# Order of the first transfers and number of filler matmuls at the head of an FFT-convolution kernel

## The chip, the cores and the metric

The kernel runs on one core of a Trainium2 chip. The metric is device time in microseconds; lower is better. The time before is the median of three runs, 264.54 us (264.13 to 264.58).

## What is computed

A circular two-dimensional convolution of one 224 x 224 image with 96 channels in and 96 out, and a 7 x 7 filter. The reference does it by Fourier transforms:

```python
H = W = 224; C = 96; K = 7
wp = jnp.pad(w, ((0, H - K), (0, W - K), (0, 0), (0, 0)))
Xf = rfft2(x, axes=(1, 2))
Wf = rfft2(wp, axes=(0, 1))
Yf = jnp.einsum('bhwi,hwio->bhwo', Xf, Wf)
y = irfft2(Yf, s=(H, W), axes=(1, 2)).astype(bfloat16)
```

## The kernel before

The kernel does not follow the reference's transform over the whole image. Rows are cut into eight blocks of 28, each with a halo of 6 rows, and a short transform (17 slots of frequencies, `NS`) runs along the rows as a matmul with a table `Fm`. Along the columns the filter's taps are applied as shifted matmuls, with combinations of taps and planes that save multiplications. The image is walked in seven tiles of 32 columns (`t` = 0 to 6).

For one tile, stage A transforms pixels (`xn` and, for the first tile, a part of `WF` that is not yet needed) to `xf`; VectorE (DVE) makes sums and differences of planes of `xf`, called `J`, in `jit`; stage B (`b_round`, 17 rounds a tile) multiplies `xf` and `J` with the transformed filter `WF` and sums into `yf`; `yf` goes through DRAM (`scr`) and comes back as `tt`, on which stage C (`c_jobs`) transforms back with a table `Gm` and stores. PSUM is one pool of eight banks, and each matmul group takes the next bank (`bank()`). Which of VectorE and ScalarE (ACT) evacuates a bank is fixed when the program is built, by a running sum of costs (`evac`).

The wrapper `_Ordered` makes each engine, and the one DMA queue that SyncE (SP) issues, execute in the order in which the program is written. So the head is an order written by hand. These are its steps:

- L178 to L192, the transfers. `xh_bufs` are the 6 halo columns left of the first tile, for each of the two halves of the image's rows (`jg` 0 and 1). `load_x(0, 0)` loads the first tile's pixels of the first half, `load_x(0, 1)` (L197) those of the second. `load_rows` issues two transfers each, 112 rows and 6. The weights go to `wq`: two transfers for the last filter tap's row, three for a third of the columns of the other 48 rows. Then four transfers copy them within the chip, from even to odd partitions of `wq`, shifted by half the output channels; each copy waits for the weight transfer whose bytes it reads.
- L199 to L208, `warm(n)`: n matmuls of a zero tile `wu`, 512 columns wide, into a bank that nobody reads. They are the fillers; `warm(8)` and `warm(9)` stand ahead of everything on TensorE.
- L231 to L347: GpSimd (POOL), VectorE and ScalarE compute the tables `Fm` and `Em` (the filter's transform, columns behind the weights in `wq`), and POOL alone goes on to the table `Gm` (`build_g`), in small operations on tiles called `ct`. Its last two steps, a sine on ACT and a product on POOL, are in `fin` (L342), which L776 calls as `g_fin()`.
- L758 to L769, TensorE's head: 12 matmuls for the halo columns of both halves (`a_bank`), 96 for the first half of the first tile (`fj[p][0]`, jobs for three groups of frequencies), then the fillers of L766, then `prep_jobs(0)`, 48 matmuls of `wq` that give the first two slots of `WF`.
- L770 to L776: the second half's first group of jobs (`fj[0][1]`, 32 matmuls), the loads of the second tile's pixels, the first planes `J` (`jit(0, 0)`), and `g_fin()`.
- From L816 on, the rounds. The first round of stage B writes `tt__557` (a PSUM copy on ACT, L567), the second `tt__676` (ACT, L604) and `u` (DVE, L607). Between the rounds' matmuls run the other `prep_jobs` and the remaining jobs of the first tile.

Of the kernel before, what the change touches and what calls it, by code (L numbers as in the profile page):

```python
# [21 lines left out]
PAD = KT - 1  # L22
# [33 lines left out]
def kernel(  # L56
# [7 lines left out]
    _, H, W, C = x.shape  # L64
# [40 lines left out]
    def bank():  # L105
        return pools["psb"].tile([128, 512], F32, name="pb")
# [5 lines left out]
    def apart(key, zone, r):  # L112
        for z, q in parts.setdefault(key, []):
            if z != zone and q.engine != r.ins.engine:
                tc.declare_no_dep(r.ins, q, reason="disjoint parts of one tile")
        parts[key].append((zone, r.ins))
        return r

    def evac(out_ap, in_ap, n):
        if tail[0]:  # L120
            return tail_evac(out_ap, in_ap, n)
        cv, ca = 180 + 1.0 * n, 160 + 0.85 * n
        if load["v"] + cv <= load["a"] + ca:
            load["v"] += cv
            return VE.tensor_copy(out=out_ap, in_=in_ap)
        load["a"] += ca
        return SE.copy(out=out_ap, in_=in_ap)
# [5 lines left out]
    def dma(out_ap, in_ap):  # L133
        return DE.dma_start(out=out_ap, in_=in_ap)
# [26 lines left out]
    xh_bufs = [late[:, 2 * (XW + 32) + i * XHW:2 * (XW + 32) + (i + 1) * XHW] for i in range(2)]  # L161
    assert 2 * (XW + 32 + XHW) <= 8 * NTAP * C and NSLOT - 8 > slot(PGRP[-1][0], 0)

    def load_rows(xb, jg, w0, npx):
        h0 = jg * HB - PAD
        n = npx * C

        def ld(p0, p1, hh):
            return dma(xb[p0:p1, 0:n], x[0, hh:hh + (p1 - p0), w0:w0 + npx, :].rearrange("h w c -> h (w c)"))
        return ld(PAD, R, h0 + PAD), ld(0, PAD, h0 % H)  # L170

    def xbuf(t, jg):
        return (xn_bufs if t else x0_bufs)[jg]

    def load_x(t, jg):
        return load_rows(xbuf(t, jg), jg, t * 2 * TW, 2 * TW)

    wsrc = w.rearrange("kh kw i o -> (kh kw) (i o)")  # L178
    for jg in range(2):
        load_rows(xh_bufs[jg], jg, W - PAD, PAD)  # L180
    load_x(0, 0)
    cuts = tuple((c * WC // 3, (c + 1) * WC // 3) for c in range(3))
    lr = PW - 1
    wp = WC // 16
# [1 line left out]
                bass.AP(wsrc.tensor, wsrc.offset + lr * WC + h * wp, [[WC, 1], [2 * wp, 8], [1, wp]])) for h in range(2)]  # L186
    for c0, c1 in cuts:
        wdma.append(dma(wqx[0:2 * lr:2, c0:c1], wsrc[0:lr, c0:c1]))
    wdma.append(dma(wqx[2 * lr + 1:PW2, 0:WC - C2].rearrange("p (a b) -> p a b", a=16),
                    wqx[2 * lr:2 * lr + 1, C2:WC].rearrange("p (a b) -> p a b", a=16)))  # L190
    for c0, c1 in cuts:
# [11 lines left out]
    def warm(n):  # L203
        pwu = bank()
        for _ in range(n):
            TE.matmul(pwu[:].rearrange("p (a b) -> p a b", a=4), lhsT=wu[:, 0:128], rhs=wur, start=True, stop=True)
# [215 lines left out]
    def a_bank(t, xf, xb, px, n, jg, pos):  # L422
        def single(ph):
            def f():
                pa = bank()
                a_mm(pa, xb, px + ph, n)
                a_put(t, xf, pa, ph, n, jg, pos)
            return f

        def pair():  # L430
            pa = psum_tile()
            for ph in range(2):
                a_mm(pa[:, ph], xb, px + ph, n)
            a_put(t, xf, pa, slice(0, 2), n, jg, pos)
        return [pair] if t > 2 and NP2 else [single(0), single(1)]
# [18 lines left out]
    def f_jobs(t, part):  # L454
        s0, s1 = SH2[part], SH2[part + 1]
        n = 2 * (s1 - s0) * JG
        nr = -(-TW * n // 512)
        e = [-(-TW * i // nr) for i in range(nr + 1)]
        fv = Fm[:, :, s0:s1].rearrange("p r s j -> p r (s j)")

        def mk_(jg, a, b, ph):
            def f():
                pa = bank()
                for k in range(b - a):
                    i = 2 * (a + k) + ph
                    TE.matmul(pa[:, k * n:(k + 1) * n], lhsT=xbuf(t, jg)[:, i * C:i * C + 128], rhs=fv, start=True, stop=True)
                xo = xf_tiles[t][0:C, ph, :, s0:s1, HALO + a:HALO + b, jg * JG:(jg + 1) * JG]
                pi = pa[0:C, 0:(b - a) * n].rearrange("c (w r s j) -> c r s w j", r=2, s=s1 - s0, w=b - a)
                return apart(("A", t), (a, jg, ph, part), evac(xo, pi, (b - a) * n))
            return f  # L470
        return [[mk_(jg, a, b, ph) for a, b in zip(e[:-1], e[1:]) for ph in range(2)] for jg in range(2)]
# [287 lines left out]
    for jg in range(2):  # L759
        for f in a_bank(0, xf0, xh_bufs[jg], 0, 3, jg, 0):  # L760
            f()
    fj = [f_jobs(0, p) for p in range(3)]
    for p in range(3):
        for f in fj[p][0]:
            f()
    for n in (9, 9, 6):  # L766
        warm(n)
    for f in prep_jobs(0):
        f()  # L769
# [202 lines left out]
```

## Time and profile before

| | us |
|---|---|
| median of three runs | 264.54 |
| the profiled execution | 264.27 |
| its span | 262.6 |
| TensorE busy in the span | 253.1 |
| DVE / ACT / POOL busy | 214.2 / 198.4 / 105.4 |
| TensorE busy in the first 20 us | 18.94 |
| granted TensorE clock, mean over the span | 0.995 |

All profile lines of this document have the operation's source line as L88, the line of the wrapper, so operations are told apart by the tiles that they write and read. In a timeline the columns are the start in us from the span's start, the time in us, the engine, the line, the operation, out<-in by the program's names, the shapes, and the number of instructions; in brackets the engine's idle time before it and what ended it. TensorE appears as PE (matmul) and PEld (weight load), SP's queue as SPq. The chain of waits gives start, time and engine of the work that ended last, followed back from the end.

TensorE's own timeline of the head:

```profile
1.06 6.81 PE L88 MATMUL pb<-wu 128*128 128x512 bf16 x17 [1.06 <-DVE ct L88]
7.71 3.41 PE L88 MATMUL pb<-Fm,WF 118*128 118x136 bf16 x108
10.96 5.34 PE L88 MATMUL pb<-wu 128*128 128x512 bf16 x24
16.14 3.16 PE L88 MATMUL pb<-wq 98*128 98x128 bf16 x48
19.14 1.10 PE L88 MATMUL pb<-Fm,WF 118*128 118x64 bf16 x32
20.69 0.51 PE L88 MATMUL pb<-WF,xf 96*128 96x96 bf16 x8 [0.46 <-ACT xf L88]
```

The ends of matmuls are modelled, so one row can end after the next begins. Up to 20.69 no row but the first has idle time before it.

### The profile page before, as it was taken

To read this page: it belongs to the slowest core of one execution; us is meant where nothing else is said; L and a number is where in the kernel's file an instruction comes from. 1 tells how busy PE (TensorE), PEld (TensorE's weight loads), DVE (VectorE), ACT (ScalarE), POOL (GpSimd) and SP (SyncE) were. 2 spreads that over 40 slices of the span, in tenths; PEclk is the share of its full clock that TensorE was granted. 3 is DMA by queue.
4 is the path that set the end of the run, shared out by engine and by line. 5 is a ranking of instruction groups with operands and counts; after the bars stand their busy time and mean duration, and the time that the engine had idled before them with its cause. 6 is when DMAs were issued, how large, how long until landed. Compare 5 with 4: busy or idle time off the path is not lost.

```text
span 262.6 us, 12208 instructions
## 1 busy us (share of the span) xinstructions
PE 253.1 (96%) x5160; PEld 234.6 (89%) x5160; DVE 214.2 (82%) x456; ACT 198.4 (76%) x500; POOL 105.4 (40%) x170
## 2 busy tenths in 40 slices
PE   8999998999999999999999999999999999999982
PEld 2779898999999999998999998999999999999961
DVE  5648899897979969977888788777977889889982
ACT  5549997659785666998988869989798886666662
POOL 7783032336355452234123322443133221556621
PEclk9999999999999999999999999999999999999997
DMA  6847110541111399888978559598958854586135
GB/s 163 237 140 194 35 49 2 167 149 47 50 47 47 117 245 192 246 234 210 279 241 218 166 137 316 166 259 188 325 201 206 216 161 149 146 141 187 55 112 177
DMA packets 41416, 43.44 MB, mean 165 GB/s; under 512 B 30836, under 2 KB 33104, under 8 KB 41362
## 3 DMA queue, kind: packets, MB, share of 16 engines
q1 hardware_dynamic: 41044, 41.98, 57.9%
q8 instruction: 40, 0.66, 1.1%
q0 software_dynamic: 192, 0.52, 0.7%
q10 hardware_dynamic: 126, 0.17, 0.2%
q14 instruction: 14, 0.11, 0.1%
HBM read 22.09 MB, written 19.66 MB: 159 GB/s over the span
## 4 chain that ended last, share of the span: by engine, by line
PE 85%; DVE 4%; ACT 4%; issue 3%; POOL 1%; DVEq 0%; ACTq 0%
PE pb L88 85%; ACT WF L88 2%; DVE WF L88 1%; ACT xf L88 1%; DVE xf L88 1%; POOL yf L88 1%; DVE J L88 1%; DVE u L88 1%; DVE v L88 0%; DVE yf L88 0%; ACT tt L88 0%; ACT tt__676 L88 0%; ACT tt__2951 L88 0%; ACT tt__557 L88 0%; DVE wu L88 0%
## 5 line engine op out<-in xcount | busy, mean ns | idle before, releaser
L88 PE MATMUL pb<-WF,J 96*128 96x96 bf16 x2782 | 160.4, 206 | 0.4 <-DVE WF L88 0.3
L88 PEld LDWEIGHTS <-J 96*128 96x128 bf16 x2782 | 136.1, 98 | 8.6 <-DVE u L88 1.5
L88 POOL TENSOR_TENSOR yf<-v,u 128x384 bf16<-128x384 f32 x70 | 69.0, 1000 | 129.8 <-issue 69.3
L88 ACT CAST xf<-pb 96x408 bf16<-96x408 f32 (+3 forms) x143 | 67.2, 489 | 9.1 <-PE pb L88 7.4
L88 PE MATMUL pb<-WF,xf 96*128 96x96 bf16 x991 | 61.7, 206 | 1.1 <-ACT xf L88 0.5
L88 DVE TENSOR_TENSOR J<-xf 96x1824 bf16<-96x1824 bf16 (+1 forms) x82 | 56.8, 732 | 0.1
L88 PEld LDWEIGHTS <-xf 96*128 96x128 bf16 x991 | 49.0, 98 | 2.0 <-issue 1.0
L88 PE MATMUL pb<-Fm,xn 118*128 118x136 bf16 (+3 forms) x640 | 45.5, 199 | 0.9 <-DVE u L88 0.8
L88 ACT CAST WF<-pb 96x480 bf16<-96x480 f32 (+1 forms) x59 | 29.0, 573 | 5.1 <-PE pb L88 5.0
L88 PE MATMUL pb<-tt,Gm 102*84 102x384 bf16 (+1 forms) x132 | 32.1, 326 | 0.0
L88 PEld LDWEIGHTS <-xn 118*128 118x128 bf16 x640 | 30.4, 97 | 1.2 <-issue 1.1
L88 ACT CAST yo<-pb 84x384 bf16<-84x384 f32 (+1 forms) x66 | 28.2, 485 | 2.9 <-PE pb L88 2.9
L88 ACT CAST J<-pb 84x384 bf16<-84x384 f32 (+1 forms) x65 | 28.0, 485 | 2.8 <-PE pb L88 2.5
L88 DVE TENSOR_TENSOR J<-J 96x912 bf16<-96x912 bf16 (+2 forms) x41 | 22.5, 548 | 0.0
L88 PE MATMUL pb<-wq 98*128 98x120 bf16 (+1 forms) x288 | 21.3, 226 | 0.0
L88 PEld LDWEIGHTS <-wq 98*128 98x128 bf16 x288 | 19.5, 148 | 0.2
L88 POOL TENSOR_TENSOR xn<-v,u 128x384 bf16<-128x384 f32 x12 | 10.9, 923 | 9.3 <-DVE J L88 6.3
L88 PE MATMUL pb<-wu 128*128 128x512 bf16 x43 | 12.7, 462 | 1.1 <-DVE ct L88 1.1
L88 DVE TENSOR_TENSOR yf<-v,u 128x384 bf16<-128x384 f32 x20 | 11.4, 568 | 0.7
L88 PEld LDWEIGHTS <-Gm 102*84 102x84 bf16 (+1 forms) x132 | 11.1, 117 | 0.8
L88 PEld LDWEIGHTS <-wu 128*128 128x128 bf16 x43 | 4.8, 115 | 7.7 <-issue 3.9
L88 DVE CAST WF<-pb 96x480 bf16<-96x480 f32 (+1 forms) x13 | 7.5, 611 | 4.8 <-PE pb L88 4.7
(404 smaller groups left out, 260.0 us busy)
## 6 DMA issues: line engine op xcount, KB each, us to landing
scr<-yf SPq DMA_DIRECT2D x30, 288.0 KB
xn<-in_x_dram SPq DMA_DIRECT2D x12, 672.0 KB
tt<-scr SPq DMA_DIRECT2D x24, 336.0 KB
out_dram<-yo SPq DMA_DIRECT2D x12, 252.0 KB
out_dram<-J SPq DMA_DIRECT2D x12, 252.0 KB
tt<-scr SPq DMA_DIRECT2D x6, 288.0 KB
WF<-in_x_dram SPq DMA_DIRECT2D x2, 672.0 KB
scr<-yf SPq DMA_DIRECT2D x6, 192.0 KB
```

Of the source, the lines that this page charges most:

```text
L88: r = fn(*a, **k)
```

## The change

The five weight transfers are issued first. Behind them come the halo columns and the first half of the first tile's pixels, then the four on-chip copies, then, unchanged, the second half. In TensorE's order, four fillers are put between the halo columns' matmuls and the first half's, and three stand ahead of `prep_jobs(0)` where there were 24. Nothing that the kernel computes changes.

```diff
     wsrc = w.rearrange("kh kw i o -> (kh kw) (i o)")
-    for jg in range(2):
-        load_rows(xh_bufs[jg], jg, W - PAD, PAD)
-    load_x(0, 0)
     cuts = tuple((c * WC // 3, (c + 1) * WC // 3) for c in range(3))
...
     for c0, c1 in cuts:
         wdma.append(dma(wqx[0:2 * lr:2, c0:c1], wsrc[0:lr, c0:c1]))
+    for jg in range(2):
+        load_rows(xh_bufs[jg], jg, W - PAD, PAD)
+    load_x(0, 0)
     wdma.append(dma(wqx[2 * lr + 1:PW2, 0:WC - C2].rearrange("p (a b) -> p a b", a=16),
...
     for jg in range(2):
         for f in a_bank(0, xf0, xh_bufs[jg], 0, 3, jg, 0):
             f()
+    warm(4)
     fj = [f_jobs(0, p) for p in range(3)]
     for p in range(3):
         for f in fj[p][0]:
             f()
-    for n in (9, 9, 6):
+    for n in (3,):
         warm(n)
     for f in prep_jobs(0):
         f()
```

## The prediction

> **What bounds the kernel now.** I read the shares first: TensorE is busy 253.1 of 262.6 us, so over most of the span a change of the head counts only if it moves the moment from which TensorE never waits again. The chain of waits, cut to the first 40 us, tells where that is.
>
> ```profile
> 1.06 16.75 PE pb L88 x173
> ...
> 21.24 0.32 ACT tt__557 L88
> 21.57 2.34 ACT WF L88 x5
> ...
> 26.58 0.49 ACT tt__676 L88
> 27.07 0.02 issue
> 27.09 0.36 DVE u L88
> 27.45 1.14 DVE WF L88 x2
> ...
> 29.32 9.33 PE pb L88 x222
> ```
>
> Up to 17.8 us TensorE sets the end, from there to 29.3 us it is ScalarE (ACT) and VectorE (DVE), and from 29.3 us TensorE again. So the head is worth what it moves at 29.32. ACT executes in program order, and its timeline shows what opens its long stretch:
>
> ```profile
> 19.57 1.07 ACT L88 CAST xf<-pb 96x512 bf16<-96x512 f32 x2
> 20.82 0.37 ACT L88 ACTIVATE ct<-ct,ct 102x84 f32<-102x84 f32 x1 [0.19 <-POOL ct L88]
> 21.24 0.32 ACT L88 COPY tt__557<-pb 128x192 f32<-128x192 f32 x1
> ```
>
> The ACTIVATE is the sine in `g_fin()` (L343, called at L776). It waited for GpSimd (POOL), though ACT's evacuations were done at 20.64. `tt__557` stands behind it, and from 21.24 to 27.06 ACT has no idle row. The third view is POOL and DVE at that place:
>
> ```profile
> 18.55 1.80 POOL L88 TENSOR_SCALAR ct<-ct 102x84 f32<-102x84 f32 x4
> 20.43 0.36 POOL L88 TENSOR_TENSOR ct<-ct,ct 102x84 f32<-102x84 f32 x1
> 21.27 1.27 POOL L88 TENSOR_TENSOR Gm<-ct,ct 102x84 bf16<-102x84 f32 x1 [0.48 <-ACT ct L88]
> 19.83 1.27 DVE L88 CAST xf<-pb 96x512 bf16<-96x512 f32 x2
> 21.21 1.50 DVE L88 TENSOR_TENSOR J<-xf 96x1824 bf16<-96x1824 bf16 x2
> ```
>
> POOL's chain, all of `build_g`, ends at 20.79. Its next operation, Gm, is again 102x84 with two inputs and takes 1.27 us where the one before took 0.36. It began 0.06 us after the first J operation of DVE, which reads two SBUF operands. So POOL stood still for some 0.9 us while J's first operation (1.1 us of the 1.50) ran. J follows at once on DVE's last evacuation (end 21.10).
>
> **The change, part by part.** (1) No transfer is added, only the order in SP's one queue changes. SP's rows:
>
> ```profile
> 0.81 2.27 SPq L88 DMA_DIRECT2D WF<-in_x_dram  x6
> 3.12 3.36 SPq L88 DMA_DIRECT2D wq<-in_w_dram  x5
> 8.65 3.16 SPq L88 DMA_DIRECT2D wq<-wq  x4
> 11.86 1.60 SPq L88 DMA_DIRECT2D WF<-in_x_dram  x2
> ```
>
> Before, SP sat 2.1 us in front of the on-chip copies, waiting for the weights. Now the five weight issues (3.36) run from 0.81 to 4.2, the six pixel issues (2.27) to 6.45, and the weights have by then mostly landed. The copies and the two issues of `load_x(0, 1)` behind them (4.8 us with their waits inside) then follow without the long stop, ending near 10 to 11 instead of 13.5.
>
> (2) Data. By the sizes of the issues: weights 882 KB, halo columns 266, first half 708, copies 877, second half 708 (KB of 1024 bytes), 3.52 MB together, which is the sum of the GB/s column from 1 to 17 us. Weights and first half, 1.90 MB, were through at 10.0 by that column; the last copy, which has to wait for them, was issued (0.5 us) by 11.81, so they had landed by 11.3. The same 1.90 MB now end with the pixels. The start loses up to 0.7 us (173 KB had moved by 3.0; the weight rows' two issues at 0.79 and 0.65 us each come first now), the middle gains as much (the DMA share was 0.71 to 0.87 between 9 and 15 us, where the copies came late). The pixels land at 11.3; bounds 10.4 (a column at 270 GB/s with no hole) and 12.5. The halo columns end 1.18 MB, 6.9 us in the column, landed 8.2 to 8.8. With the copies it is 2.80 MB: 13.9 in the column before; without the hole 13.5, and landed 0.5 to 1.4 later, 14.0 to 15.0.
>
> (3) TensorE. The 17 fillers end at 7.87 as before. It then waits for the halo columns until some 8.5 (before, no wait), runs their 12 matmuls (0.7 us by their width, of the 3.41 us of the row of 108), the 4 fillers added (4 x 222 ns, from 24 in 5.34 us: 0.9) to about 10.2, and waits for the pixels until 11.3. Then the 96 other matmuls (3.41 - 0.9 of overlap and halo: 2.5) end at 13.8, and 3 fillers (0.67) at 14.5, in place of 24 (5.34 us). `prep_jobs(0)` starts at 14.5 to 15.0, by the later of fillers and copies; it started at 16.14. I take 14.85, 1.3 us earlier; bounds 0.3 (pixels at 12.5, copies at 15.8) and 2.0. The second half lands some 1 us earlier too, because its issue does, so it does not stop the jobs behind prep, needed at 19.14 - 1.3 = 17.8 (its last byte was near 17 in the column before).
>
> (4) What is late next. All of prep and the second half's evacuations move 1.3 us up, TensorE, ACT and DVE alike. ACT then reaches the sine at 19.35 and must wait for POOL, whose 70-odd small operations depend on no transfer and stay where they are: 20.79. So even at best ACT gains 0.05 (21.19 against 21.24), and `tt__557`, the five WF evacuations and `tt__676` queue behind the sine, with DVE's u and WF and TensorE's rounds behind these. At this point the 1.3 us are hidden anyway.
>
> (5) What it starts. J starts at 21.21 - 1.3 = 19.9, inside POOL's last operations (from 18.55: four in 1.80, so they begin near 18.55, 18.9, 19.4 and 19.9; then the one at 20.43). Whether J meets the gap before the fourth or comes while it runs, one or two POOL operations have to stand behind J's 1.1 us. With J behind the fourth: 20.35 + 1.10 = 21.45, then the last one 0.36, 21.8; the sine 21.84 to 22.2; `tt__557` at 22.25, which is **1.0 us later** than 21.24. With J in front of the fourth: 19.9 + 1.1 + 0.4, J's second operation (0.4), 0.36, so 22.15, and 1.35 later. If J comes while the last one runs (20.43 to 20.79, shift 0.42 to 0.78), it is J that waits, and nothing is lost.
>
> **The sum**: head -1.3 as far as ACT's sine, of which 0.05 remains; POOL behind J +1.05; ACT, DVE and TensorE carry this unchanged to 29.32, as ACT's stretch has no idle row to absorb it: +1.0. Against the profiled execution's 264.27 us that is 265.3; the median of the three runs, 264.54, stands 0.27 above this execution, and I place the forecast between, 265.4. Its own range is 265.1 to 266.0.
>
> [...] The granted clock was 0.84 in the slice 259 to 260 us and 0.50 after it, and the last matmul ended at 257.4, so it fell 2.3 us after work stopped. [...]
>
> **The rivals.** *No change, the POOL wall alone*: the shift is under 0.8 us, J comes after or during POOL's last operation. For it: the late bounds of (2). Time 264.27 - 0.05 = 264.2. Chance 0.20. *Faster, the shift passes on*: the copies arrive early and POOL ends earlier, because DVE's casts leave it: its 102x84 operations take 0.43 under DVE's casts and the one in a DVE pause 0.26, so four of them could give 0.7. Then ACT goes on at 20.5: 263.6; with the whole 1.3 passed on, 263.0. Against it: J is a worse neighbour than the casts. Chance 0.12. *Slower, the clock*: in the waits at 7.9 and 10.2 TensorE is idle for 1.7 of 3.4 us and the clock halves, so that first-half jobs and prep run at 400 instead of 222 ns per filler, 1.8 times: 0.8 x (2.5 + 2.9) = 4.3 at most, less the 1.3 of head start: up to +3, and about 266.5 if it lasts half as long. It decides from the moment prep starts after 16.2. Chance 0.08. *Slower, late data*: the pixels behind the weights land after 13, prep starts at 16.2 to 16.8: 264.3 to 265.0. Chance 0.05. That the order does not change at all would be the first rival: the queue is one, and SP's issues follow the program's order.
>
> **How the numbers follow.** Forecast 0.55, no change 0.20, faster 0.12, clock 0.08, late data 0.05. A measurement of this kernel tells about 0.2%, 0.53 us, from no change. Slower by over that: 0.55, the clock, and a little over half of late data, 0.66; within it 0.22; faster 0.12. The range reaches from 263.9, which takes in the wall alone, to 266.2, above J in front of the fourth operation; what is left out is most of faster and of the clock.
>
> **What would show it.** SP's copies issued by about 10 us; TensorE idle before the halo columns and before the first half; prep near 14.9; J near 19.9; POOL's last ct operation stretched over 1 us; ACT idle over 2 us before the sine, which ends near 22.2; TensorE idle about 1 us longer near 29. It is wrong if the sine ends at 21.2 or before, if J starts later than 20.8, or if TensorE's long stretch starts at 29.3 or earlier.

## The result and the profile after

The changed kernel takes 266.56 us, median of six runs (265.97 to 267.44), against 264.38 us for the kernel before on the same chip: a ratio of 1.0079, interval 1.0064 to 1.0095, by which it is 2.1 us slower. The forecast was 265.4 us and its range ended at 266.2. The direction was right, but by luck: neither the cause nor the size was the forecast's.

The profiled execution (267.44 us, span 265.7) is the slowest of the six. TensorE's timeline of its head, to be laid beside the one shown above:

```profile
1.06 5.67 PE L88 MATMUL pb<-wu 128*128 128x512 bf16 x17 [1.06 <-DVE ct L88]
8.94 0.95 PE L88 MATMUL pb<-Fm,WF 118*128 118x136 bf16 x12 [2.21 <-DVE wq L88]
9.73 1.03 PE L88 MATMUL pb<-wu 128*128 128x512 bf16 x4
14.09 3.02 PE L88 MATMUL pb<-Fm,WF 118*128 118x64 bf16 x96 [3.34 <-DMA WF<-in_x_dram]
16.95 1.44 PE L88 MATMUL pb<-wu 128*128 128x512 bf16 x3
18.19 3.25 PE L88 MATMUL pb<-wq 98*128 98x128 bf16 x48
21.28 1.10 PE L88 MATMUL pb<-Fm,WF 118*128 118x64 bf16 x32
```

Before, no row here but the first had idle time ahead of it. Now TensorE waits 2.21 us for the halo columns and 3.34 us for the first half's pixels. (The first bracket names a DVE operation that happened to end then; the halo columns of the first half landed at 8.81, and with the order alone, in the first experiment below, the bracket of the same row names their transfer.) `prep_jobs(0)`, the 48 matmuls of `wq`, start at 18.19 instead of 16.14: 2.05 us later, not 1.3 earlier. The second thing to see is the last three fillers: 1.44 us for three, where 24 took 5.34. Here is why, in a view by stretches (busy time and number of instructions of TensorE, its weight loads, DVE, ACT and POOL; then the granted clock, the DMA share and GB/s):

```profile
14.00:15.00 1.00, 0.91 (x32) 0.94 (x33) 0.24 (x1) 0.48 (x1) 0.71 (x5) 1.00 0.98 242
15.00:16.00 1.00, 1.00 (x37) 1.00 (x34) 1.00 (x3) 0.92 (x3) 0.77 (x5) 0.52 1.02 246
16.00:17.00 1.00, 1.00 (x41) 1.00 (x39) 0.64 (x3) 0.74 (x2) 0.92 (x4) 0.50 1.01 233
17.00:18.00 1.00, 1.00 (x8) 0.35 (x5) 0.48 (x1) 0.58 (x1) 0.88 (x2) 0.50 0.55 154
18.00:19.00 1.00, 1.00 (x13) 0.81 (x12) 0.25 (x1) 0.00 (x0) 0.82 (x4) 0.77 0.19 59
```

The granted clock halved just after work had begun again, for 3.4 us by the trace's clock records (15.04 to 18.46). The chain of waits of the same execution, cut to the pieces that matter:

```profile
6.32 7.64 DMA WF<-in_x_dram
13.96 0.14 issue
14.09 4.89 PE pb L88 x107
...
31.46 9.37 PE pb L88 x222
```

In the chain TensorE's first stretch now hangs on the pixels' last transfer, issued at 6.32 and landed at 13.96. TensorE's long stretch begins at 31.46, where it was 29.32: 2.14 us later. The 2.05 us of prep are all but 0.1 of it, and the medians differ by as much (2.18). Of the extra 0.9 us of this one execution, against its median, 0.82 is a wait at 234.09, where stage C waits for a round trip through DRAM. And the wall on which the forecast was built is not there, in the timelines of ACT and POOL:

```profile
21.71 1.07 ACT L88 CAST xf<-pb 96x512 bf16<-96x512 f32 x2
22.67 0.37 ACT L88 ACTIVATE ct<-ct,ct 102x84 f32<-102x84 f32 x1
23.39 0.32 ACT L88 COPY tt__539<-pb 128x192 f32<-128x192 f32 x1 [0.34 <-PE pb L88]
23.12 0.38 POOL L88 TENSOR_TENSOR Gm<-ct,ct 102x84 bf16<-102x84 f32 x1 [2.32 <-ACT ct L88]
```

The sine follows ACT's evacuations without a wait, since POOL was done at 20.81, and Gm takes 0.38 us, not 1.27, as it now runs ahead of J (23.35).

### The profile page after: what moved, and what is told of

It is laid out like the page before. It is cut to its first block, busy times and chain, and to the rows that moved or that the text cites. A ratio compares the mean times of both kernels' runs of the same rounds, so it can differ in the third digit from the quotient of the medians.

```text
span 265.7 us, 12169 instructions
## 1 busy us (share of the span) xinstructions
PE 250.0 (94%) x5143; PEld 233.0 (88%) x5143; DVE 214.2 (81%) x456; ACT 198.7 (75%) x500; POOL 104.5 (39%) x170
## 4 chain that ended last, share of the span: by engine, by line
PE 76%; DMA 6%; ACT 5%; issue 4%; DVE 4%; SPq 2%; POOL 1%; DVEq 0%; POOLq 0%; ACTq 0%
PE pb L88 76%; DMA WF<-in_x_dram 3%; ACT WF L88 3%; SPq L88 2%; DMA scr<-yf 2%; DMA tt<-scr 1%; DVE WF L88 1%; POOL yf L88 1%; ACT xf L88 1%; DVE xf L88 1%; DVE J L88 1%; DVE u L88 1%; DVE v L88 0%; DVE yf L88 0%; ACT tt L88 0%
## 5 line engine op out<-in xcount | busy, mean ns | idle before, releaser
L88 DVE CAST xf<-pb 96x512 bf16<-96x512 f32 (+3 forms) x17 | 9.9, 599 | 5.1 <-PE pb L88 5.1
L88 PE MATMUL pb<-Fm,WF 118*128 118x64 bf16 (+3 forms) x204 | 7.3, 191 | 5.5 <-DMA WF<-in_x_dram 3.3
L88 PEld LDWEIGHTS <-WF 118*128 118x128 bf16 x204 | 6.7, 101 | 6.6 <-DMA WF<-in_x_dram 6.5
L88 DVE TENSOR_TENSOR yf<-v,u 128x384 bf16<-128x384 f32 x20 | 11.3, 567 | 0.7
```

The costliest lines, as they stand in the source:

```text
L88: r = fn(*a, **k)
```

## The experiments

All times are medians, each beside runs of the kernel before on the same chip in the same session (264.32 to 264.45 us). "Prep" is the start of the 48 matmuls of `wq`; "long stretch" is the start of TensorE's uninterrupted run (29.32 before).

**The order alone, and the fillers alone.** The first kernel has the new order with the fillers of before:

```diff
-    warm(4)
     fj = [f_jobs(0, p) for p in range(3)]
...
-    for n in (3,):
+    for n in (9, 9, 6):
```

> New order of the transfers, fillers as before (17 and 24, none between). Late data: the first half's last bytes land near 14 us as in the changed kernel, the 96 matmuls end near 17, 24 fillers behind them take 5.3 us (up to 10 if the clock is halved), so prep starts at 22 to 24 instead of 18.2: 270 to 274 us. If instead the fillers were the cause and the order harmless, prep stays near 16.1 and the time near 264.4.

270.57 us, ratio 1.0238 (1.0205 to 1.0272). Prep at 22.32, long stretch at 35.50: the pixels landed at 13.5, the clock halved from 13.31 to 16.73, and 24 fillers stood behind them. So the order is harmful by itself, and the fillers had to go with it.

The second has the order of before with the new fillers:

```diff
+    warm(4)
     fj = [f_jobs(0, p) for p in range(3)]
...
-    for n in (9, 9, 6):
+    for n in (3,):
```

> Order of the transfers as before, fillers of the changed kernel (17, 4 and 3). Late data: pixels in time at 7.9, the fillers end near 12.5, prep waits for the copies, which land at 15.3, and starts 0.8 us earlier than before; no time is lost. My forecast's POOL theory on top: J then starts near 20.4, beside POOL's last operations; POOL's chain cannot end before 20.8, so the time is 264.4 (no gain) to 265.4 (J locks POOL out). Pass-on rival: the 0.8 us come through, 263.6. Clock: TensorE idles from 12.5 to 15.3, and if that halves the clock prep takes 5 instead of 3 us: 266.

266.41 us, ratio 1.0077 (1.0051 to 1.0104): as slow as the whole change. Two rows of this kernel's TensorE timeline, and three of its stretches, in the columns of the table above, show it:

```profile
11.49 0.81 PE L88 MATMUL pb<-wu 128*128 128x512 bf16 x3
15.78 5.26 PE L88 MATMUL pb<-wq 98*128 98x128 bf16 x48 [3.48 <-DMA wq<-wq]
```

```profile
13.00:14.00 1.00, 0.00 (x0) 0.00 (x0) 0.00 (x0) 0.00 (x0) 0.73 (x5) 1.00 0.91 197
14.00:15.00 1.00, 0.00 (x0) 0.00 (x0) 0.00 (x0) 0.00 (x0) 0.71 (x5) 0.52 0.79 283
...
19.00:20.00 1.00, 1.00 (x12) 1.00 (x11) 0.56 (x1) 0.63 (x3) 0.83 (x3) 0.50 0.00 0
```

Prep begins 0.36 us earlier than before, but at half clock it takes 5.26 us instead of 3.16, and the long stretch starts at 31.04, 1.72 late. It is the clock rival of the expectation that came true. What the fillers of before bought was the clock, not the time that they filled.

**The clock kept in the changed kernel.**

```diff
-    warm(4)
+    warm(19)
```

> The changed kernel with 19 fillers instead of 4 between the halo columns and the first half, to cover the wait for the pixels. Late data: the pixels still land near 14 and the copies near 17.7; with the clock kept, the 96 matmuls take 2.5 instead of 3.0 us and the three fillers 0.67 instead of 1.44, so prep waits for the copies at 17.7 to 17.8 instead of 18.2: 0.4 us less than the changed kernel, 266.2. Clock as the main cause: prep back to about 16.5, time near 264.8.

265.95 us, ratio 1.0053 (1.0034 to 1.0073); 0.6 us of the changed kernel's loss are gone. The two intervals overlap, so the times alone don't show this; the traces do, by the start of prep.

```profile
9.76 4.27 PE L88 MATMUL pb<-wu 128*128 128x512 bf16 x19
14.03 2.70 PE L88 MATMUL pb<-Fm,WF 118*128 118x64 bf16 x96
16.58 0.81 PE L88 MATMUL pb<-wu 128*128 128x512 bf16 x3
17.59 3.19 PE L88 MATMUL pb<-wq 98*128 98x128 bf16 x48 [0.20 <-DMA wq<-wq]
```

These are rows of TensorE's timeline of this kernel. With the clock whole, what ends last in front of prep is the copies (landed at 17.45), and prep starts at 17.59, 0.60 us before the changed kernel's 18.19. The remaining 1.45 us are the data's.

**Nothing close behind the pixels.** The changed kernel, its copies held until the first half has landed:

```diff
-    load_x(0, 0)
+    x00 = load_x(0, 0)
...
+    for d in wdma[5:]:
+        for q in x00:
+            tc.add_manual_dep(d.ins, q.ins.name, SYNC, reason="copies behind the first half")
```

> The changed kernel, with the four on-chip copies made to wait until the first half of the pixels has landed. If the pixels are late only because they stand behind the weights, they land near 14 as now, and the copies move out to 18 or later: slower by 1 us or more than the changed kernel. If the copies issued close behind take bandwidth from the DMA engines that lag with the pixels, the pixels land near 12 to 12.5, 1.5 us earlier, and the copies are no later than 17.

270.73 us, ratio 1.0234 (1.0189 to 1.0279). The copies then land at 19.5, and the clock halves from 17.60 to 24.43, so that prep is both late and slow; the long stretch starts at 34.80. Two rows of its TensorE timeline:

```profile
12.30 2.69 PE L88 MATMUL pb<-Fm,WF 118*128 118x64 bf16 x96 [1.49 <-DMA WF<-in_x_dram]
19.64 5.14 PE L88 MATMUL pb<-wq 98*128 98x128 bf16 x48 [4.00 <-DMA wq<-wq]
```

The pixels land at 12.16 instead of 13.96, from the same place in the queue behind the same bytes. In the five kernels that have this order and transfers queued close behind, they land between 13.2 and 14.0, so these cost 1.0 to 1.8 us. Both halves of the expectation were partly right: the pixels came early as its second half has it, but the copies, expected there at 17 at the latest, came later than 18, as in its first.

**What is queued behind, from DRAM instead of on-chip.** The changed kernel with the odd rows of `wq` read from DRAM a second time:

```diff
...
-        wdma.append(dma(wqx[1:2 * lr:2, max(c0 - C2, 0):c1 - C2], wqx[0:2 * lr:2, max(c0, C2):c1]))
+        wdma.append(dma(wqx[1:2 * lr:2, max(c0 - C2, 0):c1 - C2], wsrc[0:lr, max(c0, C2):c1]))
```

(and the last row alike)

> The changed kernel, with the odd rows of the weights loaded from DRAM a second time instead of copied within the chip; same bytes, same place in the queue, no wait for the first load. If whatever is queued close behind takes bandwidth from the engines that lag, the pixels still land near 13.5 to 14 and the time stays near 266.5. If it is the on-chip copies in particular, the pixels land near 12, as they do when the copies are held back, the odd rows near 15, prep starts near 15.5 to 16 and the time is near 264.4.

266.18 us, ratio 1.0061 (1.0041 to 1.0082). The pixels land at 13.2, the odd rows at 16.6; the clock halves again and prep starts at 17.56. That is nearer to the 13.3 to 14.0 with copies behind than to the 12.16 with nothing, so it is not the on-chip copies in particular. The same edit in the kernel before was to show whether the odd rows come earlier there:

> The kernel before with the odd rows loaded from DRAM a second time instead of copied; no wait of SP for the first load. The fillers still set prep at 16.14, so the time stays at 264.4; what is read is when the odd rows land: 15.3 as the copies do, or earlier by the hole in the queue, near 14.

264.31 us, ratio 0.9996 (0.9984 to 1.0009), and they land at 15.6: no earlier. Something else in this trace bears on the forecast. SP does not stop for the weights here, and the last weights land at 12.29, where they land between 10.94 and 11.29 in the seven other kernels with the order of before.

**The second half held behind the copies.** The same question one place later in the queue, on the changed kernel with 19 fillers:

```diff
-    load_x(0, 1)
+    for q in load_x(0, 1):
+        for d in wdma[5:]:
+            tc.add_manual_dep(q.ins, d.ins.name, SYNC, reason="second half behind the copies")
```

> As e3_keep_clock (changed order, 19 fillers ahead of the first half), with the second half's two transfers waiting until the copies have landed. The same theory: the pixels are late as before (13.5 to 14, the copies still stand close behind them), the copies land near 16 to 16.5 instead of 17.5, prep starts 0.7 us earlier than 17.59; the second half lands near 20, 0.5 us late at most; 265.3 to 266. If the copies' lateness comes from the pixels ahead of them alone, they land at 17.5 as before and the time rises to 266.5.

266.58 us, ratio 1.0076 (1.0058 to 1.0094). The copies land at 15.98 instead of 17.45, so 1.5 us of their lateness was the load behind them. Prep did not start 0.7 us earlier, as expected, but at 17.35, behind the pixels' jobs and fillers, and the second half, needed next, came 1.02 us late. In the order of before, with 18 fillers and the late sine (below):

> As e6_trim_late_sine (order of before, sine late), with 18 fillers instead of 20 ahead of the first two filter slots, and the second half's two transfers made to wait until the four copies have landed. If what is queued close behind a transfer makes its last bytes late, the copies land near 14 to 14.5 instead of 15.3 to 15.5, and prep starts at 15.0 or earlier (18 fillers end near 14.9); the second half then lands near 18 to 18.5, at most 0.5 us late for its jobs, so 263.4 to 264.0. If the copies land at 15.3 all the same, the holding only makes the second half late: 264.3 to 265.

267.07 us, ratio 1.0088 (1.0058 to 1.0119). Copies at 14.68, a little past what was expected, and prep at 14.92, as the theory has it; but the second half, expected near 18.5, lands at 19.8, and TensorE waits 1.83 us. The profiled run took 264.82 at a mean clock of 0.997; the other five 266.4 to 267.9 at 0.981 to 0.988, so there the wait cost clock as well.

**The POOL wall, on the kernel before.** Four fillers fewer, nothing else:

```diff
-    for n in (9, 9, 6):
+    for n in (9, 9, 2):
```

> The kernel before with 20 fillers ahead of the first two filter slots instead of 24, order unchanged: prep starts 0.7 to 0.8 us earlier (15.3 to 15.5, when the copies land). POOL theory of the forecast: the sine on ScalarE still ends at 21.2, because POOL's chain ends at 20.8; the time stays at 264.3 to 264.4, no gain. Pass-on rival: 0.7 us faster, 263.7.

264.35 us, ratio 0.9993 (0.9983 to 1.0003): no gain. ACT's timeline of this kernel:

```profile
19.05 1.07 ACT L88 CAST xf<-pb 96x512 bf16<-96x512 f32 x2
20.84 0.37 ACT L88 ACTIVATE ct<-ct,ct 102x84 f32<-102x84 f32 x1 [0.72 <-POOL ct L88]
21.11 0.30 ACT L88 COPY tt__553<-pb 128x192 f32<-128x192 f32 x1
```

ACT's evacuations end 0.5 us earlier than before and the sine stands where it stood (20.84 against 20.82), now with 0.72 us of waiting for POOL ahead of it. Prep gained 0.54 us; the long stretch, at 29.09, gained 0.23. Then the sine moved off that place, with its tiles in a pool that lives on:

```diff
...
-    g_fin()
     stmp_cm.__exit__(None, None, None)
...
+        if r == 4:
+            g_fin()
```

> As e5_trim, with the sine and product of g_fin called at round 4 instead of ahead of round 0. POOL theory: ScalarE no longer waits for POOL, the 0.7 us pass on, 263.7, so 0.6 to 0.7 below e5_trim. Pass-on rival (the sine never held anything): the same as e5_trim, at most 0.4 below it, the sine's own time.

264.05 us, ratio 0.9988 (0.9974 to 1.0001), short of the 263.7 expected. Here the copies landed at 15.53 and prep started at 15.77, so 0.37 us were gained there and not 0.7; of these, 0.32 arrive at the long stretch (29.00). The times alone do not part the two kernels; the rows of the trace do.

**A short gap.** The kernel before with 14 fillers ahead of prep instead of 24:

> Order of the transfers as before, 14 fillers instead of 24 ahead of the first two filter slots: TensorE is done at 14.0 and waits for the copies until 15.4, a gap of 1.4 us instead of the 3.5 us of e2_fillers_only. If the clock halves only after a long gap, this is e5_trim over again: mean clock 0.994 to 0.998, 264.3 to 264.4. [...]

266.14 us, ratio 1.0055 (1.0036 to 1.0073), mean clock 0.992 or 0.993 in all five runs. In the profiled run the copies came at 16.66, so the gap was 2.62 us, not 1.4, in its TensorE timeline:

```profile
16.90 4.05 PE L88 MATMUL pb<-wq 98*128 98x128 bf16 x48 [2.62 <-DMA wq<-wq]
```

The clock halved, from 18.73 to 22.14. How short a gap is safe stays open.

**The best version.** Two fillers fewer than before (22) and the late sine:

> As e6_trim_late_sine with 22 fillers instead of 20, so that TensorE has no gap ahead of the copies' landing: prep starts at 15.7, 0.4 us earlier than before, and with the sine late this passes on: 263.9 to 264.1, 0.3 to 0.4 us below the kernel before. If the sine's wait had not mattered, it would be the same 0.4 us.

263.94 us, ratio 0.9979 (0.9964 to 0.9995): 0.5 us faster than the kernel before, and the whole interval lies below 1. Prep starts at 15.81 behind the fillers with no wait, and the long stretch at 28.97. The trace explains 0.35 us of it, which the interval holds. No run has 22 fillers with the sine in its old place, so what the sine adds here is not shown by itself.

## Why the prediction was wrong

- **What bounds the kernel**: right. The head counts by when the long stretch begins; where no later wait, half clock or POOL wall comes between, prep's shift arrives there unchanged (2.05 and 2.14 us in the changed kernel, 6.18 and 6.18 with the order alone, 1.45 and 1.47 with the clock kept).
- **Step (2), the data, is the step that failed**: "The pixels land at 11.3; bounds 10.4 [...] and 12.5." They landed at 13.96. I had moved over the time at which the same 1.90 MB had landed in the kernel before (11.3, 1.3 us after the GB/s column had passed them), and had put the cost of what is queued behind the pixels at nothing. The column did pass 1.90 MB near 10.85 us. But TensorE waits for the last of 16 DMA engines, and with the copies queued right behind, the leading engines went on to these while the lagging ones still had pixels: the main transfer's engines landed from 11.05 to 13.45, and the first landing of a copy is at 11.45. Holding the copies back brought the end to 12.16, inside the bounds. SP's long stop before the copies, which I counted as a hole to be gained, had kept what follows off the transfers ahead: without it, in the order of before, the last weights landed a microsecond later (12.29).
- **The same step, the start**: "up to 0.7 us" lost and "the middle gains as much". 92 KB had moved by 4.0 us against 383, which is 1.1 us at the 270 GB/s of the five slices that follow, and from 9 to 16 us the engines were busy at 0.96 to 1.07 and moved only 204 to 252 GB/s. With nothing behind them the copies land at 14.7 in the old order and 16.0 in the new: 1.3 us are the order's, and the load behind adds 0.6 to 0.9 in five runs of the old (2.0 in a sixth) and 1.0 to 1.7 in three runs of the new (17.00, 17.45, 17.70).
- **Step (3)** fell with it: prep at 18.19, not 14.85. Its first wait was long, 2.21 us against some 0.6, also because the 17 fillers were done at 6.73 and not at 7.87; the first record of the full clock is at 4.80 in this run, 7.10 in the run before.
- **Step (4), the POOL wall**: right as a mechanism of this kernel, shown by the trimmed kernel's 0.72 us row and by the late sine, but it never came into play in the changed kernel.
- **Step (5), J locking POOL out**: not reached. No run put J ahead of POOL's last chain operation; in the trimmed kernel J came during it (20.68), and that operation kept its 0.37 us, as the forecast says for that case. The 1.0 us priced there was not measured.
- **The rivals**: "late data" (0.05) and "the clock" (0.08) both happened, the first setting off the second. Late data was priced at 264.3 to 265.0 and cost 1.45 us by itself; the clock was priced at up to 3 us and cost 0.6, as most of the halved stretch lay on the pixels' jobs and fillers while the copies were still under way. No run shows the condition that the clock rival puts, 1.7 us of idle time in the 3.4 from 7.9 to 11.3; the drops came at gaps of 2.45 to 4.00 us. I had treated the two rivals as separate cases, and that the new waits are the clock's cause made them one. That the clock rival names 266.5 us is luck: its own sum for half the time, 264.27 + 2.15 - 1.3, gives 265.1. And the reason given for the "faster" rival does not hold: with the order alone VectorE was idle from 17.69 to 22.77, and three of POOL's four 102x84 operations in question still took 0.42 to 0.43 us. POOL's chain ended between 20.78 and 20.88 in all fourteen kernels.

## What to carry to other kernels

Date a transfer that an engine waits for by its slowest DMA engine (13.96 here), not by the bytes moved (10.85), and ask what is queued right behind it, which cost 1.0 to 1.8 us here; so put what is needed first at the front, and try to leave the queue thin behind the transfer that ends a wait. Count fillers ahead of a wait as the price of the clock: here removing them alone cost 2 us, in the work behind the gap. And before shortening a head, look which other engine's chain ends at the same place: here 0.23 of 0.54 us came through with the sine in its place, and 0.32 of 0.37 with it moved.

## What the runs showed that I had not expected

The clock halved in the head of six kernels, at gaps of TensorE of 2.45 to 4.00 us, while a gap of 2.81 us ahead of the halo columns (the changed order with the second half held) brought no drop. It stayed halved for 3.41 us in the changed kernel and in the run with the 2.62 us gap, 3.42 with the order alone and 6.83 with the copies held back. In the run with the 2.62 us gap the 3.42 us before the drop, 15.31 to 18.73, still held 1.83 us of matmuls, 54%; in the profiled run with the 1.83 us gap (mean clock 0.997) the 3.41 us from 15.77 to 19.18 were busy for 67% and nothing fell. Of the six drops, only the one with the order alone follows 3.4 us without a matmul. But no busy share of such a stretch tells when the clock falls: in the changed kernel the 3.41 us from 8.22 to 11.63 were busy for 53%, and the clock stayed whole. What the condition is stays open.

And on a crowded queue the slowest engine was 2.4 us behind the fastest for one transfer of 672 KB (1.5 to 3.1 in the five kernels with something close behind), against 0.9 to 1.8 us for the same transfer in the eight that had it at the front.
